# First FFN product in three token slices of 512 instead of four of 384

## The chip, the cores and the metric

The kernel runs on one core of one Trainium2 chip. The metric is the device time of one execution in microseconds (us), the median of three runs. About 0.2%, some 2 us, is what such a measurement can tell from no change.

## What is computed

An attention with a decaying state makes `x` (3072 tokens by 512). Two feed-forward blocks follow; the change touches the second one:

```python
def _moe2_ref(x, w_in, w_out):          # w_in 512 x 2048, w_out 2048 x 512
    h = x @ w_in
    g = h * (1.0 / (1.0 + np.exp(-1.702 * h)))
    return (g @ w_out).astype(np.float32)
```

## The kernel before

Two devices shape every matrix product. First, each operand is split into a high part, rounded to the fp32r format, and a low part that holds the rest, and one product is three matmuls: high by high, high by low, low by high (`mm3`; the profile's lines L259, L260, L261). Second, a two-by-two block product is done with seven block products instead of eight (P1 to P7, after Strassen and Winograd), which costs sums and differences on the vector engine (DVE).

The program runs in stages on the tensor engine (PE): attention and the first gates, the mixed weights, the "blend" (the first block's output, written to the spools `yd`), the expand stage (class `Expand`: `x @ w_in` and the gate, result to the spools `gd`), and the contract stage (`contract`: `g @ w_out`). The order on each engine is the order in which the Python code issues, so what stands before what is decided by hand.

Expand runs over token slices (`run`, L657), and in each over eight quads (`quad`, L630). A quad takes one column block of `w_in` (a "left operand": seven parts of 256 columns, each as high and low) and the slice's seven right operands, and makes the products in the order P1, P5, P4 of the quad before, P6, P2, P7, P3. Each product is six matmuls. ACT copies the sum out of PSUM after P1 (`s1`), P5 (`s5`), P6 (`u2`) and P7 (`u3`), and the next product on the same bank waits for that copy. DVE adds P2, P7 and P3 into `s1`, `u3`, `u2`. The generator `fourth` (L610) finishes the quad before: two gates on ACT (`g0`, `b12`) in front of P4, two behind it, four differences on DVE (L624), and a store to `gd`.

The seven right operands of a slice are made by the generator `operands` (L508): the slice's raw tokens are loaded, four differences are taken (`sub`), and `split` makes a high part (a cast) and a low part (a subtraction) for each of P1, P5, P6, P2, P7, P3, P4. `step(at)` in `run` moves it on by one part at places written as (quad, quarter): `NEXT0` and `NEXT` (L689, L690) in the slice before, and (0, 0), (0, 1) in the slice itself. Those of the first slice are made beside the blend (`ahead`).

Left operands sit in homes (`slot`, L558): left 0 in a home of its own, lefts 1 to 7 in seven others. As they fall free in the last slice, `OPENING` (L755) loads and splits the first operands of contract into them: `opening_slot`, `opening_split`, and `split_w` for the weights of P1. Contract has 21 turns of 48 matmuls, all of 512 columns; its loads from `gd` (`load`, L699) and its stores (`store`, L770) cut 512 tokens where a slice of 384 ends.

Of the kernel before, what the change touches and what calls it, by code (L numbers as in the profile page):

```python
# [16 lines left out]
P = 128  # L17
# [11 lines left out]
TS = 384  # L29
NS = NT // (2 * TS)  # L30
TU = 256
# [16 lines left out]
def tile_kernel(  # L48
# [36 lines left out]
    gd = spool("gd", NS, P, NQ, 7, TS)  # L85
# [413 lines left out]
    def load_y(raw, s):  # L499

        at = 0
        while at < 2 * TS:
            i, t0 = divmod(2 * TS * s + at, TB)
            n = min(TB - t0, 2 * TS - at)
            nc.sync.dma_start(raw[:, :, at : at + n], yd[i][:, :, t0 : t0 + n])
            at += n

    def operands(s, pool):  # L508

        raw = pool.tile([P, KD, 2 * TS], F32, tag="raw", name="yr")  # L510
        load_y(raw, s)
        (b11, b12), (b21, b22) = (
            [raw[:, 2 * k : 2 * k + 2, h * TS : (h + 1) * TS] for h in range(2)]
            for k in range(2)
        )
        x = right[s] = {}
        yield

        def split(name, b):
            hi, lo = (  # L520
                pool.tile([P, 2, TS], F32R, tag=f"y{w}", bufs=9, name=f"y{w}") for w in "hl"
            )
            nc.vector.tensor_copy(hi, b)
            nc.vector.tensor_tensor(lo, b, hi.bitcast(F32), ALU.subtract)
            x[name] = hi, lo

        def sub(out, a, b):
            nc.vector.tensor_tensor(out, a, b, ALU.subtract)

        t = pool.tile([P, 2, TS], F32, tag="t", name="yt")  # L530
        sub(t, b12, b11)
        sub(b12, b22, b12)
        yield
        split("P1", b11)
        yield
        split("P5", t)
        yield
        sub(t, b22, t)
        sub(b11, b21, t)
        yield  # L540
        split("P6", t)
        yield
        split("P2", b21)
        yield
        split("P7", b12)
        yield
        split("P3", b22)
        yield
        split("P4", b11)
        yield  # L550
# [4 lines left out]
    SLOT = "e", 0, 1, 4, 2, 3, 5, 6  # L555
    pools = {True: spare}

    def slot(n, shape):  # L558
        x = SLOT[n]
        return pools[x == "e"].tile(shape, F32R, tag=f"op{x}", name="op")  # L560
# [16 lines left out]
    class Expand:  # L577
# [4 lines left out]
        def bank(self, kind):  # L582
            bufs = {"a": 3, "e": 2, "c": 2}[kind]
            return self.ps.tile([P, TB], F32, tag=kind, bufs=bufs, name=kind)[:, :TS]

        def copy(self, ps, name):
            t = (
                self.ready.pop()
                if self.ready
                else self.p.tile([P, TS], F32, tag="s", bufs=6, name=name)  # L590
            )
            nc.scalar.copy(t, ps)
            return t

        def product(self, ps, name, s, j, start=False):
            xh, xl = right[s][name]
# [7 lines left out]
        def result(self, j):  # L604
            return [
                self.p.tile(shape, F32, tag=f"{tag}{j % 2}", name=tag)
                for tag, shape in (("g", [P, 7, TS]), ("b", [P, TS]))
            ]

        def fourth(self):  # L610
            a, s, j, g, b12, s1, u2, u3 = self.open
# [6 lines left out]
            for x, y, z in (  # L618
                (3, b12, g[:, 0]),
                (5, g[:, 2], b12),  # L620
                (4, g[:, 2], g[:, 3]),
                (6, g[:, 1], g[:, 4]),
            ):
                nc.vector.tensor_tensor(g[:, x], y, z, ALU.subtract)  # L624
# [5 lines left out]
        def quad(self, s, j, step):  # L630
            a, e, c = (self.bank(x) for x in "aec")
            g, b12 = self.results.pop(0) if self.results else self.result(j)
            self.product(a, "P1", s, j, True)
            s1 = self.copy(a, "s1")
# [20 lines left out]
            self.open = a, s, j, g, b12, s1, u2, u3  # L655

        def run(self):  # L657
            self.open = nxt = None
            for n in sorted(range(1, NQ), key=lambda n: SLOT[n]):
                left_tile(n)  # L660
            for n in range(1, NQ - 1):
                fetch_left(n, nc.sync)
            self.results = [self.result(0)]
            self.ready = [self.p.tile([P, TS], F32, tag="s", bufs=6, name="s1")]
            self.results.append(self.result(1))
            split_left(1, nc.vector.tensor_copy)
            for s in range(NS):

                for j in range(NQ):

                    def step(at):
                        nonlocal nxt
                        more = s + 1 < NS
                        if more and (j, at) == (2, 3):
                            nxt = operands(s + 1, self.py)
                            next(nxt)
                        elif more and (j, at) in (NEXT if s else NEXT0):
                            next(nxt)
                        elif s and (j, at) in ((0, 0), (0, 1)):
                            next(nxt)  # L680
                        if not more and (j, at) in OPENING:
                            for run in OPENING[j, at]:
                                run()

                    self.quad(s, j, step)
# [3 lines left out]
    NEXT0 = (4, 3), (6, 0), (6, 2), (6, 3), (7, 0), (7, 2), (7, 3)  # L689
    NEXT = (4, 3), (5, 1), (5, 3), (6, 3), (7, 0), (7, 2), (7, 3)  # L690
# [8 lines left out]
    def load(n, a, b, t):  # L699
        name, i = turns[n]  # L700
        low.setdefault(n, []).append((a, b, t))
        at = 0
        while at < TB:
            s, t0 = divmod(i * TB + at, TS)
            m = min(TB - at, TS - t0)
            nc.sync.dma_start(
                t[:, :, at : at + m].bitcast(F32),
                gd[s][:, a:b, RIGHT[name], t0 : t0 + m],
            )
            at += m  # L710
# [30 lines left out]
    def opening_slot(n):  # L741
        t = slot(n, [P, KH + 2, TB])
# [18 lines left out]
    for k, at in enumerate(  # L761
        ((3, 1), (3, 2), (3, 3), (4, 0), (4, 1), (4, 3), (5, 1), (5, 3))
# [3 lines left out]
    def contract(p, ps):  # L766
# [3 lines left out]
        def store(x, h, i, q, value):  # L770
            t = p.tile([P, TB], F32, tag="o", bufs=4, name="c")
            last = (x, h, i, q) == (1, 0, 2, 1)
            if not last:
                add(t, *value)
            at = 0
            while at < TB:
                s, t0 = divmod(i * TB + at, TS)
                m = min(TB - at, TS - t0)
                to = s * 2 * TS + h * TS + t0
                rows = slice((2 * x + q) * P, (2 * x + q + 1) * P)  # L780
                part = slice(at, at + m)
                if last:
                    add(t[:, part], *(v[:, part] for v in value))
                queue = nc.scalar if last and at else nc.sync
                queue.dma_start(out[rows, to : to + m], t[:, part])
                at += m

        u = [p.tile([P, 3, 2, TB], F32, name="ua")]
        for n, (name, i) in enumerate(turns):
# [4 lines left out]
            if name == "P5" and i == 0:  # L794
                u += [slot(x, [P, 3, 2, TB]).bitcast(F32) for x in (2, 3)]
# [12 lines left out]
            if i == 1 and r + 1 < 7:  # L808
                split_w(turns[n + 2][0], (7, 5)[r % 2])
# [146 lines left out]
    with tc.manual_schedule():  # L956
# [180 lines left out]
        def ahead(n):  # L1137
# [7 lines left out]
            elif early is None:  # L1145
# [4 lines left out]
                early = operands(0, py)  # L1150
# [14 lines left out]
        with tc.tile_pool(name="f", bufs=1, reuse_waits="tile") as pools[False]:  # L1165
# [6 lines left out]
            with (  # L1172
                tc.tile_pool(name="f2", bufs=1, side="right", reuse_waits="tile") as p2,
                tc.tile_pool(name="psf2", bufs=1, space=PSUM, reuse_waits="tile") as ps2,
            ):
                contract(p2, ps2)
# [100 lines left out]
```

## Time and profile before

| what | us |
|---|---|
| median of three runs (973.81 to 975.08) | 974.02 |
| the profiled execution | 973.11 |
| its span, first to last instruction | 971.3 |
| expand stage in it, first to first matmul of contract | 504.53 to 738.16 |
| contract stage, first to last matmul | 738.16 to 966.45 |

Matmuls are pipelined: the profile's duration of one is longer than the distance from one start to the next, and the second is what a stream costs. "Busy" of the tensor engine therefore also covers short waits; they are seen as larger distances between starts.

### The profile page before, as it was taken

Reading aid. Unit: us, or ns where it says so; the run is one execution under the profiler, and the core shown is the slowest. Engines: PE = TensorE matmul, PEld = TensorE weight load, DVE = VectorE, ACT = ScalarE, POOL = GpSimd, SP = SyncE. Lnnn points to the kernel's source line nnn. Section 1 sums busy time; section 2 is a strip of 40 time slices with the busy share of each in tenths; the row PEclk is TensorE's granted clock in tenths of the full one; section 3 lists DMA queues with packets and bytes.
Section 4 is the critical chain, followed back from the end, with each engine's and each line's share of the span. In section 5 each row is a group of like instructions: output and inputs, shape, how many; then the busy total and the mean of one; then the engine's idle time right before and its main releaser. Section 6 shows DMA issues by size and latency. Waiting matters only on the chain.

```text
span 971.3 us, 15570 instructions
## 1 busy us (share of the span) xinstructions
PE 952.3 (98%) x5992; PEld 826.0 (85%) x5992; DVE 719.3 (74%) x943; ACT 424.4 (44%) x691; POOL 229.4 (24%) x281
## 2 busy tenths in 40 slices
PE   6899999999999999999999999999999999999998
PEld 5678778888888888888889999999998888888886
DVE  6898878889889886766687976948686665566662
ACT  4555444433222222654536654554555544353430
POOL 6422100478787875330020000000000000000000
PEclk9999999999999999999999999999999999999999
DMA  9999766579898999899778546464696968767871
GB/s 349 400 350 350 281 214 202 199 246 359 314 365 288 357 338 395 306 334 312 248 254 305 226 171 246 203 250 184 253 348 252 339 222 271 254 196 230 290 233 50
DMA packets 112618, 266.74 MB, mean 275 GB/s; under 512 B 7872, under 2 KB 67264, under 8 KB 103456
## 3 DMA queue, kind: packets, MB, share of 16 engines
q1 hardware_dynamic: 96560, 186.64, 54.8%
q0 software_dynamic: 15840, 78.91, 21.4%
q8 instruction: 47, 0.77, 0.3%
q14 instruction: 27, 0.22, 0.1%
q10 hardware_dynamic: 144, 0.20, 0.1%
HBM read 164.53 MB, written 101.19 MB: 274 GB/s over the span
## 4 chain that ended last, share of the span: by engine, by line
PE 90%; DVE 4%; DMA 3%; issue 1%; ACT 1%; POOL 0%; DVEq 0%; POOLq 0%; ACTq 0%; SPq 0%
PE m L259 12%; PE m L260 12%; PE m L261 12%; PE psm L261 7%; PE psm L260 7%; PE psm L259 7%; PE a L260 4%; PE a L261 4%; PE a L259 4%; PE e L260 2%; PE e L259 2%; PE e L261 2%; PE psg L259 2%; PE y L442 2%; PE s L376 1%; DMA raw<-in_w_dram 1%
## 5 line engine op out<-in xcount | busy, mean ns | idle before, releaser
L260 PE MATMUL psm<-xl,wh 128*128 128x512 f32 x320 | 124.5, 389 | 0.0
L259 PE MATMUL psm<-xh,wh 128*128 128x512 f32 x320 | 124.5, 389 | 0.0
L261 PE MATMUL psm<-xh,wl 128*128 128x512 f32 x320 | 124.5, 389 | 0.0
L261 PE MATMUL m<-h,op 128*128 128x512 f32 x320 | 124.5, 389 | 0.0
L259 PE MATMUL m<-h,op 128*128 128x512 f32 x320 | 124.5, 389 | 0.0
L260 PE MATMUL m<-l,op 128*128 128x512 f32 x304 | 118.3, 389 | 0.0
L726 ACT CAST h<-l 128x2048 fp32r<-128x2048 f32 x38 | 72.3, 1914 | 85.1 <-PE m L261 56.9
L727 DVE TENSOR_TENSOR l<-l,h 128x2048 fp32r<-128x2048 f32 x38 | 85.7, 2286 | 22.5 <-ACT h L726 22.5
L732 POOL DMA_DIRECT2D op<-sw x6 | 3.2, 532 | 393.0 <-PE a L261 212.7
L260 PE MATMUL a<-yl,op 128*128 128x384 f32 x256 | 85.6, 335 | 0.1
L259 PE MATMUL a<-yh,op 128*128 128x384 f32 x256 | 85.5, 334 | 0.0
L261 PE MATMUL a<-yh,op 128*128 128x384 f32 x256 | 85.5, 334 | 0.0
L141 ACT ACTIVATE x<-raw 128x512 f32<-128x512 f32 x72 | 46.9, 675 | 70.3 <-DMA raw<-in_wo_dram 35.7
L261 PEld LDWEIGHTS m<-h,op 128*128 128x128 f32 x320 | 60.1, 188 | 12.6
L260 PEld LDWEIGHTS psm<-xl,wh 128*128 128x128 f32 x320 | 60.1, 188 | 12.6
L259 PEld LDWEIGHTS psm<-xh,wh 128*128 128x128 f32 x320 | 60.1, 188 | 12.5
L259 PEld LDWEIGHTS m<-h,op 128*128 128x128 f32 x320 | 60.1, 188 | 12.4
L261 PEld LDWEIGHTS psm<-xh,wl 128*128 128x128 f32 x320 | 60.1, 188 | 12.3
L260 PEld LDWEIGHTS m<-l,op 128*128 128x128 f32 x304 | 57.1, 188 | 11.8
L259 PE MATMUL m<-h,wh 128*128 128x512 f32 x168 | 65.4, 389 | 0.0
L261 PE MATMUL m<-h,wl 128*128 128x512 f32 x168 | 65.4, 389 | 0.0
L175 DVE TENSOR_TENSOR l<-l,h 128x2048 fp32r<-128x2048 f32 x19 | 43.6, 2292 | 26.1 <-ACT h L274 24.6
(172 smaller groups left out, 2198.1 us busy)
## 6 DMA issues: line engine op xcount, KB each, us to landing
gd<-g SPq DMA_DIRECT2D x32, 1344.0 KB, 5.0
qkv<-in_qkv_dram POOLq DMA_DIRECT2D x20, 1024.0 KB, 9.2
l<-gd SPq DMA_DIRECT2D x26, 768.0 KB, 7.4
l<-hd SPq DMA_DIRECT2D x19, 1024.0 KB, 7.4
raw<-in_w_dram SPq DMA_DIRECT2D x30, 512.0 KB, 5.9
hd<-g POOLq DMA_DIRECT2D x12, 1280.0 KB, 7.2
raw<-in_wo_dram SPq DMA_DIRECT2D x24, 512.0 KB, 6.8
l<-gd SPq DMA_DIRECT2D x24, 512.0 KB, 5.2
```

The lines of the kernel that those rows point to most:

```text
L141: nc.scalar.activation(x, high, AF.Abs, scale=2.0**16)
L175: nc.vector.tensor_tensor(lo, x, hi.bitcast(F32), ALU.subtract)
L259: nc.tensor.matmul(ps, wh, xh, start=start, stop=False, skip_group_check=True)
L260: nc.tensor.matmul(ps, wh, xl, start=False, stop=False, skip_group_check=True)
L261: nc.tensor.matmul(ps, wl, xh, start=False, stop=stop, skip_group_check=True)
L376: nc.tensor.matmul(self.s[u * D : (u + 1) * D, j, p, t], qkt[c][r, 1, p, u * D : (u + 1) * D], qkt[c][r, 0, p, t], start=True, stop=True, ...
L442: nc.tensor.matmul(out_y, vs[c][:, 2 * p + j, :], pt[c][:, j, p, :], start=(c % NCK == 0 and p < 2), stop=True, skip_group_check=True,)
L726: nc.scalar.copy(hi, x.bitcast(F32))
L727: nc.vector.tensor_tensor(x, x.bitcast(F32), hi.bitcast(F32), ALU.subtract)
L732: queue.dma_start(t.bitcast(F32), sw[PART[name]])
```

## The change

Expand works in three slices (`NS = 3`) of 512 tokens per half instead of four of 384. The raw tokens are loaded as four blocks into four tiles that are homes of low parts, and P1, P2, P7 and P3 leave their low parts there (`Homes` hands tags out and takes back those of the slice before). For the second and third slice the high parts are cast on ACT instead of DVE, in other places. Lefts 0 and 7 share one home, so each is fetched and split again (`FETCH`, `SPLIT`), and the order of the quads is `QUADS`. `g` is stored in two pieces of three and four parts. Contract's loads and stores need no cutting.

```diff
-TS = 384
-NS = NT // (2 * TS)
+NS = NT // (2 * TB)
...
-    def operands(s, pool):
+    def operands(s, copy, pool):
...
-            nc.vector.tensor_copy(hi, b)
+            htag, hi = ys_homes.tile("h")
+            tag, lo = low
+            copy(hi, b)
             nc.vector.tensor_tensor(lo, b, hi.bitcast(F32), ALU.subtract)
...
+        raws = [ys_homes.tile("l") for _ in range(4)]
+        b11, b12, b22, b21 = (whole(t) for t in raws)
+        for b, (k, h) in zip((b11, b12, b22, b21), ((0, 0), (0, 1), (1, 1), (1, 0))):
+            nc.sync.dma_start(b, yd[2 * s + h][:, 2 * k : 2 * k + 2])
+        yield
+        t, t7 = (pool.tile([P, 2, TB], F32, tag=f"yt{n}", name="yt") for n in range(2))
         sub(t, b12, b11)
         yield
+        sub(t7, b22, b12)
         yield
+        split("P1", b11, raws[0])
         yield
+        give("P1", "P5")
+        split("P5", t, ys_homes.tile("l"))
+        sub(t, b22, t)
         yield
+        split("P6", t, ys_homes.tile("l"))
+        sub(t, b21, t)
+        give("P6")
         yield
+        give("P2", "P7", "P3", "P4")
+        split("P2", b21, raws[3])
+        split("P7", t7, raws[1])
         yield
+        split("P3", b22, raws[2])
         yield
+        split("P4", t, ys_homes.tile("l"))
         yield
...
-    SLOT = "e", 0, 1, 4, 2, 3, 5, 6
+    SLOT = "e", 0, 1, 4, 2, 3, 5, "e", "w"
...
+            nc.sync.dma_start(gd[s][:, j, :3], g)
+            t = self.value("t", 4)
...
-            nc.sync.dma_start(gd[s][:, j], g)
-            if s == 0 and j == 0:
-                fetch_left(NQ - 1, nc.sync)
+            nc.sync.dma_start(gd[s][:, j, 3:], t)
+            if n in FETCH:
+                left_tile(FETCH[n])
+                fetch_left(FETCH[n], nc.sync)
...
-            if s == 0 and j + 2 < NQ:
-                split_left(j + 2)
+            if n in SPLIT:
+                split_left(SPLIT[n])
...
-                            nxt = operands(s + 1, self.py)
+                            nxt = operands(s + 1, nc.scalar.copy, self.py)
                             next(nxt)
-                        elif more and (j, at) in (NEXT if s else NEXT0):
+                        elif (more and at in NEXT) or (s and at in ((0, 0), (0, 1), (0, 2))):
                             next(nxt)
...
-    NEXT0 = (4, 3), (6, 0), (6, 2), (6, 3), (7, 0), (7, 2), (7, 3)
-    NEXT = (4, 3), (5, 1), (5, 3), (6, 3), (7, 0), (7, 2), (7, 3)
+    QUADS = range(NQ), range(NQ - 1, -1, -1), (0, 1, 2, 3, 7, 4, 5, 6)
+    FETCH = {0: 7, NQ: 0, 2 * NQ: 7}
+    SPLIT = {j: j + 2 for j in range(NQ - 2)} | {NQ + 4: 0, 2 * NQ + 2: 7}
+    NEXT = (4, 3), (5, 3), (6, 0), (7, 0), (7, 1)
...
-    OPENING = {(n + 1, 1): [lambda n=n: opening_slot(n)] for n in range(4)}
-    OPENING[5, 1] = [lambda: load_w("P1", 4)]
+    OPENING = {(n + 2, 1): [lambda n=n: opening_slot(n)] for n in range(3)}
+    OPENING[5, 1] = [lambda: opening_slot(3)]
+    OPENING[6, 1] = [lambda: load_w("P1", 4)]
     for n in range(2):
-        OPENING[6, 1 + 2 * n] = [
+        OPENING[7, 1 + 2 * n] = [
             lambda n=n: split_w("P1", 5, n * KH, n * KH + KH, nc.vector.tensor_copy)
```

How the order moves, at three places. First ACT in the first quad of the second slice (`yh` is a high part, `yl` holds a raw token block or a low part, `yt` a difference). Before:

```order
L592 COPY s5_5428<-e_5410 128x384
L602 ACTIVATE g_5333<-s1_5341 128x384
L602 ACTIVATE b_5334<-u2_5369 128x384
L592 COPY u2_5448<-a_5409 128x384
L602 ACTIVATE g_5333<-u3_5391 128x384
L602 ACTIVATE g_5333<-a_5330 128x384
L592 COPY u3_5474<-a_5409 128x384
```

Now:

```order
L607 COPY s5_5445<-e_5429 128x512
L617 ACTIVATE g1_5447<-s1_5358 128x512
L617 ACTIVATE b_5448<-u2_5389 128x512
L529 CAST yh_5457<-yl_5055 128x1024
L529 CAST yh_5460<-yt_5203 128x1024
L607 COPY u2_5469<-a_5428 128x512
L617 ACTIVATE g1_5447<-u3_5418 128x512
L617 ACTIVATE g1_5447<-a_5349 128x512
L529 CAST yh_5480<-yl_5054 128x1024
L607 COPY u3_5496<-a_5428 128x512
```

The casts for P2 and P7 stand between the gate `b` and the copy `u2`, and the one for P3 in front of `u3`. The second place is DVE at the same turn, from an add of the last quad of the first slice on. Before (P2's, P7's and P3's parts in this order):

```order
L650 TENSOR_TENSOR u3_5391<-u3_5391,s5_5349 128x384
L523 CAST yh_5394<-yr_5040 128x768
L524 TENSOR_TENSOR yl_5395<-yr_5040,yh_5394 128x768
L653 TENSOR_TENSOR u2_5369<-e_5331,u2_5369 128x384
L523 CAST yh_5405<-yr_5040 128x768
L524 TENSOR_TENSOR yl_5406<-yr_5040,yh_5405 128x768
L523 CAST yh_5438<-yr_5040 128x768
L524 TENSOR_TENSOR yl_5439<-yr_5040,yh_5438 128x768
L624 TENSOR_TENSOR g_5333<-b_5334,g_5333 128x384
```

Now, from the low part of P6 in that last quad on:

```order
L530 TENSOR_TENSOR yl_5400<-yt_5202,yh_5401 128x1024
L534 TENSOR_TENSOR yt_5202<-yl_5055,yt_5202 128x1024
L659 TENSOR_TENSOR s1_5358<-c_5351,s1_5358 128x512
L662 TENSOR_TENSOR u3_5418<-u3_5418,s5_5366 128x512
L665 TENSOR_TENSOR u2_5389<-e_5350,u2_5389 128x512
L530 TENSOR_TENSOR yl_5055<-yl_5055,yh_5457 128x1024
L530 TENSOR_TENSOR yl_5053<-yt_5203,yh_5460 128x1024
L636 TENSOR_TENSOR t_5474<-b_5448,g1_5447 128x512
L636 TENSOR_TENSOR t_5474<-g1_5447,b_5448 128x512
L636 TENSOR_TENSOR t_5474<-g1_5447,t_5474 128x512 x2
L530 TENSOR_TENSOR yl_5054<-yl_5054,yh_5480 128x1024
```

Both parts of P2 stood before the last add of the old slice, and those of P7 and P3 right behind it, all ahead of the gates' differences; now the low parts of P2 and P7 come after all three adds, and P3's after the four differences `t`. The third place is DVE at the end of expand, where the weights of contract's P1 are split in two halves. Before, both halves are done with a whole quad to come:

```order
L738 CAST op_7041<-op_6968 128x1024
L739 TENSOR_TENSOR op_6968<-op_6968,op_7041 128x1024
L624 TENSOR_TENSOR g_7000<-b_7001,g_7000 128x384
L624 TENSOR_TENSOR g_7000<-g_7000,b_7001 128x384
L624 TENSOR_TENSOR g_7000<-g_7000 128x384 x2
L647 TENSOR_TENSOR s1_7080<-c_7071,s1_7080 128x384
L650 TENSOR_TENSOR u3_7126<-u3_7126,s5_7088 128x384
L653 TENSOR_TENSOR u2_7104<-e_7070,u2_7104 128x384
```

Now they stand in the last quad itself, the second behind its last add:

```order
L744 CAST op_6596<-op_6521 128x1024
L745 TENSOR_TENSOR op_6521<-op_6521,op_6596 128x1024
L659 TENSOR_TENSOR s1_6559<-c_6552,s1_6559 128x512
L662 TENSOR_TENSOR u3_6612<-u3_6612,s5_6567 128x512
L665 TENSOR_TENSOR u2_6585<-e_6551,u2_6585 128x512
L744 CAST op_6596<-op_6521 128x1024
L745 TENSOR_TENSOR op_6521<-op_6521,op_6596 128x1024
```

## Rows read from the trace of the kernel before

**Rows 1.** Busy time by stretch: expand, then contract (columns named in the first row)

```profile
core 0: us, PE busy (x) PEld busy (x) DVE busy (x) ACT busy (x) POOL busy (x), PEclk, DMA share, GB/s
...
504.50:738.20 233.70, 233.59 (x1346) 232.98 (x1345) 175.70 (x301) 123.69 (x260) 1.44 (x3) 1.00 0.63 242
738.20:971.30 233.10, 228.64 (x1009) 188.97 (x1007) 132.85 (x96) 94.64 (x63) 2.65 (x5) 1.00 0.71 236
```

**Rows 2.** Timeline of PE: start, duration, engine, line, what; expand, then contract

```profile
504.53 0.33 PE L259 MATMUL a<-yh,op 128*128 128x384 f32 x1
...
555.69 0.33 PE L260 MATMUL e<-yl,op 128*128 128x384 f32 x1
...
567.99 0.34 PE L259 MATMUL e<-yh,op 128*128 128x384 f32 x1
...
571.35 0.34 PE L259 MATMUL a<-yh,op 128*128 128x384 f32 x1
571.80 0.44 PE L260 MATMUL a<-yl,op 128*128 128x384 f32 x1
572.08 0.34 PE L261 MATMUL a<-yh,op 128*128 128x384 f32 x1
...
738.16 0.39 PE L259 MATMUL m<-op 128*128 128x512 f32 x1
...
966.45 0.39 PE L261 MATMUL m<-h,op 128*128 128x512 f32 x1
```

**Rows 3.** Timeline of DVE at the first turn between slices

```profile
570.20 0.55 DVE L523 CAST yh<-yr 128x768 fp32r<-128x768 f32 x1
570.79 0.96 DVE L524 TENSOR_TENSOR yl<-yr,yh 128x768 fp32r<-128x768 f32 x1
571.66 0.55 DVE L647 TENSOR_TENSOR s<-c,s 128x384 f32<-128x384 f32 x1
```

**Rows 4.** Groups of ACT in expand: total us, mean ns of one

```profile
L592 ACT COPY u<-a 128x384 f32<-128x384 f32 x64 | 30.7, 480 | 41.5 <-PE a L261 41.5
L602 ACT ACTIVATE g<-u 128x384 f32<-128x384 f32 x32 | 17.0, 531 | 0.0
...
L726 ACT CAST h<-op 128x1024 fp32r<-128x1024 f32 x1 | 1.0, 1041 | 0.0
L953 ACT COPY c<-m 128x512 f32<-128x512 f32 x1 | 0.6, 589 | 2.1 <-PE m L261 2.1
```

**Rows 5.** Groups of DVE in expand

```profile
L624 DVE TENSOR_TENSOR g<-b,g 128x384 f32<-128x384 f32 x32 | 17.8, 555 | 28.1 <-ACT b L602 28.1
...
L753 DVE TENSOR_TENSOR op<-op 128x512 fp32r<-128x512 f32 x8 | 5.5, 692 | 0.3
...
L739 DVE TENSOR_TENSOR op<-op 128x1024 fp32r<-128x1024 f32 x2 | 2.5, 1225 | 0.1
L738 DVE CAST op<-op 128x1024 fp32r<-128x1024 f32 x2 | 1.4, 684 | 0.0
```

**Rows 6.** Timeline of ACT at the first turn

```profile
571.61 0.48 ACT L592 COPY s<-e 128x384 f32<-128x384 f32 x1 [0.56 <-PE e L261]
...
573.18 0.53 ACT L602 ACTIVATE b<-u 128x384 f32<-128x384 f32 x1 [0.40 <-DVE u L653]
574.04 0.48 ACT L592 COPY u<-a 128x384 f32<-128x384 f32 x1 [0.33 <-PE a L261]
574.41 0.53 ACT L602 ACTIVATE g<-u 128x384 f32<-128x384 f32 x1
```

**Rows 7.** DMA issues in expand: KB each, median us from issue to landing

```profile
gd<-g SPq DMA_DIRECT2D x31, 1344.0 KB, 5.0
op<-sp SPq DMA_DIRECT2D x4, 896.0 KB, 8.2
```

**Rows 8.** Timeline of DVE late in the blend, low part of its next operand

```profile
485.39 2.29 DVE L175 TENSOR_TENSOR l<-l,h 128x2048 fp32r<-128x2048 f32 x1 [1.63 <-ACT h L274]
```

**Rows 9.** Timeline of SP's queue at the end of expand

```profile
741.00 0.32 SPq L625 DMA_DIRECT2D gd<-g  x1
745.91 0.37 SPq L706 DMA_DIRECT2D l<-gd  x1
```

**Rows 10.** Timeline at the end of the program

```profile
966.88 0.76 DVE L768 TENSOR_TENSOR c<-m,ua 128x128 f32<-128x128 f32 x2 [4.75 <-PE m L261]
...
967.66 0.37 ACTq L785 DMA_DIRECT2D out_dram<-c  x1
```

More of the change, by code (lines that the diff above doesn't have):

```diff
@@ L84, in tile_kernel @@
     yd = spool("yd", NB, P, KD, TB)
-    gd = spool("gd", NS, P, NQ, 7, TS)
+    gd = spool("gd", NS, P, NQ, 7, TB)
     sp = spool("sp", NQ, P, 7 * 256)
@@ L497, in tile_kernel, with __init__, add, tile @@
     right = {}
[L499 to L506, printed above, removed]
-    def operands(s, pool):
[L510 to L515, printed above, removed]
-        x = right[s] = {}
[L517 to L522, printed above, removed]
-            nc.vector.tensor_copy(hi, b)
+    class Homes:
+        def __init__(self):
+            self.pools = {}
+            self.free = dict(l=[], h=[])
+        def add(self, pool, **counts):
+            for w, n in counts.items():
+                for _ in range(n):
+                    tag = f"y{w}{len(self.pools)}"
+                    self.pools[tag] = pool
+                    self.free[w].append(tag)
+        def tile(self, w):
+            tag = self.free[w].pop(0)
+            return tag, self.pools[tag].tile([P, 2, TB], F32R, tag=tag, name=f"y{w}")
@@ L524, in split, with give @@
+    ys_homes = Homes()
+    def operands(s, copy, pool):
+        x = right[s] = {}
+        used = {n: tags for n, (_, tags) in right.get(s - 1, {}).items()}
+        def give(*names):
+            for n in names:
+                for w, tag in zip("hl", used.get(n, ())):
+                    ys_homes.free[w].append(tag)
+        def split(name, b, low):
+            htag, hi = ys_homes.tile("h")
+            tag, lo = low
+            copy(hi, b)
             nc.vector.tensor_tensor(lo, b, hi.bitcast(F32), ALU.subtract)
-            x[name] = hi, lo
+            x[name] = (hi, lo), (htag, tag)
@@ L527, in sub, with whole @@
         def sub(out, a, b):
             nc.vector.tensor_tensor(out, a, b, ALU.subtract)
-        t = pool.tile([P, 2, TS], F32, tag="t", name="yt")
+        def whole(low):
+            return low[1].bitcast(F32)
+        raws = [ys_homes.tile("l") for _ in range(4)]
[4 more added lines that the diff above has]
+        t, t7 = (pool.tile([P, 2, TB], F32, tag=f"yt{n}", name="yt") for n in range(2))
@@ L553, in tile_kernel @@
     PART = dict(P1=0, P2=1, P4=2, P5=3, P6=4, P7=5, P3=6)
-    SLOT = "e", 0, 1, 4, 2, 3, 5, 6
-    pools = {True: spare}
+    SLOT = "e", 0, 1, 4, 2, 3, 5, "e", "w"
+    pools = {"e": spare}
     def slot(n, shape):
         x = SLOT[n]
-        return pools[x == "e"].tile(shape, F32R, tag=f"op{x}", name="op")
+        return pools.get(x, pools.get("f")).tile(shape, F32R, tag=f"op{x}", name="op")
     def left_tile(n):
@@ L583, in bank, with value, copy @@
             bufs = {"a": 3, "e": 2, "c": 2}[kind]
[L584 to L591, printed above, removed]
+            return self.ps.tile([P, TB], F32, tag=kind, bufs=bufs, name=kind)
+        def value(self, tag, *shape):
+            return self.p.tile([P, *shape, TB], F32, tag=tag, name=tag)
+        def copy(self, ps, tag):
+            t = self.value(tag)
             nc.scalar.copy(t, ps)
@@ L595, in product @@
         def product(self, ps, name, s, j, start=False):
-            xh, xl = right[s][name]
+            xh, xl = right[s][name][0]
             for k in range(2):
@@ L602, in gated @@
             nc.scalar.activation(x, c, AF.Gelu_apprx_sigmoid)
[L604 to L608, printed above, removed]
         def fourth(self):
-            a, s, j, g, b12, s1, u2, u3 = self.open
+            a, s, j, n, s1, u2, u3 = self.open
+            g, b12 = self.value(f"g{n % 2}", 3), self.value("b")
             self.gated(g[:, 0], s1)
@@ L617, in fourth, with quad @@
             self.gated(g[:, 1], a)
+            nc.sync.dma_start(gd[s][:, j, :3], g)
+            t = self.value("t", 4)
             for x, y, z in (
[L619 to L622, printed above, removed]
-            ):
-                nc.vector.tensor_tensor(g[:, x], y, z, ALU.subtract)
-            nc.sync.dma_start(gd[s][:, j], g)
-            if s == 0 and j == 0:
-                fetch_left(NQ - 1, nc.sync)
+                (0, b12, g[:, 0]),
+                (2, g[:, 2], b12),
+                (1, g[:, 2], t[:, 0]),
+                (3, g[:, 1], t[:, 1]),
+            ):
+                nc.vector.tensor_tensor(t[:, x], y, z, ALU.subtract)
+            nc.sync.dma_start(gd[s][:, j, 3:], t)
+            if n in FETCH:
+                left_tile(FETCH[n])
+                fetch_left(FETCH[n], nc.sync)
             yield
-        def quad(self, s, j, step):
+        def quad(self, s, j, n, step):
             a, e, c = (self.bank(x) for x in "aec")
-            g, b12 = self.results.pop(0) if self.results else self.result(j)
             self.product(a, "P1", s, j, True)
-            s1 = self.copy(a, "s1")
+            s1 = self.copy(a, f"s{n % 2}")
             self.product(e, "P5", s, j, True)
@@ L654, in quad @@
             step(3)
-            self.open = a, s, j, g, b12, s1, u2, u3
+            self.open = a, s, j, n, s1, u2, u3
         def run(self):
             self.open = nxt = None
-            for n in sorted(range(1, NQ), key=lambda n: SLOT[n]):
+            for n in sorted(range(1, NQ - 1), key=lambda n: SLOT[n]):
                 left_tile(n)
@@ L662, in run @@
                 fetch_left(n, nc.sync)
-            self.results = [self.result(0)]
-            self.ready = [self.p.tile([P, TS], F32, tag="s", bufs=6, name="s1")]
-            self.results.append(self.result(1))
+            for tag in ("s1", "s5", "u2", "u3", "s0", "b"):
+                self.value(tag)
+            for tag, m in (("t", 4), ("g0", 3), ("g1", 3)):
+                self.value(tag, m)
+            ys_homes.add(self.p, l=3, h=1)
             split_left(1, nc.vector.tensor_copy)
-            for s in range(NS):
-                for j in range(NQ):
+            for s, order in enumerate(QUADS):
+                for at_j, j in enumerate(order):
                     def step(at):
                         nonlocal nxt
+                        at = at_j, at
                         more = s + 1 < NS
-                        if more and (j, at) == (2, 3):
-                            nxt = operands(s + 1, self.py)
+                        if more and at == (2, 3):
+                            nxt = operands(s + 1, nc.scalar.copy, self.py)
                             next(nxt)
-                        elif more and (j, at) in (NEXT if s else NEXT0):
+                        elif (more and at in NEXT) or (s and at in ((0, 0), (0, 1), (0, 2))):
                             next(nxt)
[L679 to L682, printed above, removed]
+                        if not more:
+                            for run in OPENING.get(at, ()):
                                 run()
-                    self.quad(s, j, step)
+                    self.quad(s, j, s * NQ + at_j, step)
             for _ in self.fourth():
                 pass
-    NEXT0 = (4, 3), (6, 0), (6, 2), (6, 3), (7, 0), (7, 2), (7, 3)
-    NEXT = (4, 3), (5, 1), (5, 3), (6, 3), (7, 0), (7, 2), (7, 3)
+    QUADS = range(NQ), range(NQ - 1, -1, -1), (0, 1, 2, 3, 7, 4, 5, 6)
+    FETCH = {0: 7, NQ: 0, 2 * NQ: 7}
+    SPLIT = {j: j + 2 for j in range(NQ - 2)} | {NQ + 4: 0, 2 * NQ + 2: 7}
+    NEXT = (4, 3), (5, 3), (6, 0), (7, 0), (7, 1)
     RIGHT = dict(P1=0, P2=1, P3=2, P5=3, P6=4, P7=5, P4=6)
@@ L741, in opening_slot @@
     def opening_slot(n):
-        t = slot(n, [P, KH + 2, TB])
+        t = slot((1, 2, 3, 7)[n], [P, KH + 2, TB])
         if n < 2:
@@ L772, in store @@
             last = (x, h, i, q) == (1, 0, 2, 1)
[L773 to L786, printed above, removed]
+            to = (2 * i + h) * TB
+            rows = slice((2 * x + q) * P, (2 * x + q + 1) * P)
+            for part in (slice(0, 384), slice(384, TB)) if last else (slice(0, TB),):
+                add(t[:, part], *(v[:, part] for v in value))
+                queue = nc.scalar if last and part.start else nc.sync
+                queue.dma_start(out[rows, to + part.start : to + part.stop], t[:, part])
         u = [p.tile([P, 3, 2, TB], F32, name="ua")]
@@ L794, in contract @@
             if name == "P5" and i == 0:
-                u += [slot(x, [P, 3, 2, TB]).bitcast(F32) for x in (2, 3)]
+                u += [slot(x, [P, 3, 2, TB]).bitcast(F32) for x in (3, 7)]
             pq = [ps.tile([P, TB], F32, tag="m", bufs=6, name="m") for _ in range(2)]
@@ L808, in contract @@
             if i == 1 and r + 1 < 7:
-                split_w(turns[n + 2][0], (7, 5)[r % 2])
+                split_w(turns[n + 2][0], (8, 5)[r % 2])
             for q, m in enumerate(pq):
@@ L1149, in ahead @@
                 )
-                early = operands(0, py)
+                ys_homes.add(py, l=8, h=7)
+                early = operands(0, nc.vector.tensor_copy, py)
                 next(early)
@@ L1163, in tile_kernel @@
         first.close()
-        with tc.tile_pool(name="f", bufs=1, reuse_waits="tile") as pools[False]:
+        with tc.tile_pool(name="f", bufs=1, reuse_waits="tile") as pools["f"]:
             with (
@@ L1175, in tile_kernel @@
             ):
+                pools["w"] = p2
                 contract(p2, ps2)
```

23 lines of the change are left out of this document (2 added, 21 removed).

## The prediction

> **What bounds the kernel now.** I read the stretches first. In expand PE is busy 233.59 of 233.70 us, DVE 175.70, ACT 123.69, at a granted clock of 1.00 [rows 1]: PE sets the time, DVE has a quarter to spare. Busy time hides short waits, so I read PE's starts next [rows 2]. From 555.69 to 567.99 lie 71 starts, 12.30 us: a 384-column matmul costs 0.1732 us. In contract, 1008 matmuls of 512 columns go from 738.16 to 966.45: 228.29 over 1007 steps, 0.2267 us each. Expand's 1344 matmuls would need 232.8 us; they take 738.16 - 504.53 = 233.6. The rest is waits: at 571.35 the next start comes 0.45 later instead of 0.17, and the one behind it 0.28 later, so a wait also costs some 0.1 of resuming. What it waits for is on DVE [rows 3]: the low part of P4 starts at 570.79, lasts 0.96, ends at 571.75, and the matmul that reads it starts 0.05 later. So already now, where the slice turns, the operands come just too late. This is the place to look at.
>
> **Fewer matmuls.** 128 columns more cost 0.0535 us, 0.418 ns each, so 384 columns are 160 ns and some 13 ns belong to each instruction. The columns stay the same (4 x 384 = 3 x 512), 336 instructions go: 1008 x 0.2267 = 228.5 us, against the 233.6 of today **-5.1 us**, with the old waits in it. The Trainium skill ("TensorE: Matmul & The Clock Gate", Back-to-back issue gap) gives a warm gap of N / 2.4 + 2.5 ns for isolated matmuls; by that the 336 instructions are worth an estimated 0.8 us, not 4.5. Both of my pitches are measured in streams of this kernel, so they decide.
>
> **The turn between slices.** A product is now 6 x 0.2267 = 1.36 us, a quad seven of them, 9.52. Durations: ACT casts 128x1024 in 1.04, copies 512 columns in 0.59; a gate of 384 takes 0.53 against 0.48 for a copy, so I estimate 0.64 at 512 [rows 4]. DVE takes 1.23 for 128x1024, 0.69 for 512 columns, 0.68 for a 1024 cast [rows 5]. An ACT copy starts 0.26 after the product's last step (571.35, 571.61) [rows 2, 6]. The next operation on ACT starts 0.1 before the end of the one ahead (574.04 + 0.48 against 574.41) [rows 6], on DVE 0.08 (570.79 + 0.96 against 571.66), or 0.04 after it where it needs its result (570.20 + 0.55 against 570.79) [rows 3].
>
> Last quad of the old slice, from its start: P5 ends at 2.72, so ACT copies `s5` at 2.97, gates from 3.45 to 4.6, casts P5's high part 4.53 to 5.57. DVE makes its low part 5.60 to 6.83, the next difference to 7.97, the four `t` from 7.88 to 10.5 (the last reads the one ahead of it, 0.1 more), P6's low part 10.42 to 11.65, the last difference to 12.78, then the adds into `s1` at 12.70, `u3` at 13.31, `u2` at 13.92 to 14.61. That is **5.09 after the new slice's first quad has started**, since this quad holds four operations of 1.23 us for the operands beside its own eight.
>
> First quad of the new slice, from its start. PE: P1, P5, the old P4, P6, and P2 due at 5.44. ACT: the gate `b` needs `u2`, so 5.13 to 5.77 (as now it waits for DVE at 573.18 [rows 6]); then P2's cast 5.67 to 6.71, P7's 6.61 to 7.65, the copy `u2` to 8.14, two gates, P3's cast 9.1 to 10.1. DVE: P2's low part 6.74 to 7.97, P7's to 9.11, four `t` from 9.03 to 11.65, P3's low part 11.57 to 12.80. So on PE:
>
> - P2's first matmul waits for the high part from 5.44 to 6.76: 1.3 us.
> - Its second, due at 6.99, waits for the low part to 8.02: 1.0 us. P2 ends at 9.15. P7 finds its parts and `u2` there and ends at 10.51.
> - P3's first starts at 10.51; its second, due at 10.74, waits for the low part to 12.85: 2.1 us. P3 ends at 13.98, not 9.52.
>
> With 0.1 of resuming twice a turn costs 4.7 us, two turns **+9.3 us**. Bounds from below: if the gates' lateness and the `t` block came away entirely (ACT free to cast at 4.5, low part at 5.6 to 6.8), P2 would still lose 1.2 us a turn, +2.4. From above: 0.3 us of extra hand-over at each of five steps of the chain, +12. I take the chain, all from durations of this trace.
>
> P4's low part, late today, follows P3's, is ready some 1.1 us into the second quad and due at 2.7; so it costs nothing, and DVE has caught up by that quad's end.
>
> **The end of expand.** The second half of P1's weights is split in the last quad behind its last add: the four `t` end at 8.86, first half 8.78 to 10.72, adds to 12.55, second half 12.47 to 14.41. Contract begins at 9.52 + 1.36 = 10.88 and reads that low part in its fifteenth matmul, at 14.05: **+0.5 us** with resuming (0 to 1). The first store piece of the last `g` goes out at about 3.4 after contract's start, the load of the third turn stands behind the `t` piece, at 6.1, and behind the first's landing, at 8.4. Today it is issued 7.75 after 738.16 and 4.9 after the store [rows 9]; its reader is two turns of 10.9 us away, so nothing.
>
> **What I cost at nothing.** The operands of the first slice are made beside the blend by DVE as before, a third longer, two splits at once in one step: 3.8 us instead of 1.5 against an idle of 1.63 [rows 8], so one low part of the blend starts some 0.6 later; without that cover 0 to 0.7. Lefts 0 and 7 are loaded twice more, 8.2 us each [rows 7]. The tight one, 7 in the third slice, is issued 8.9 into the second quad and lands 7.6 into the third, where ACT would cast it at 7.2; the copy `u3` behind it is due at 12.2, so a landing up to 10 is hidden. Contract loads the same bytes in fewer pieces. At the end the 384 columns are now added and stored before the 128: both adds take the same 0.76 and only the last store, on ACT's queue, is smaller [rows 10]; 0 to -0.3.
>
> **Sum.** -5.1 + 9.3 + 0.5 = +4.7 us. The profiled execution (973.11, 1.8 outside its span) would be 977.8; it stood 0.9 under the median of 974.02, so I forecast **978.7**.
>
> **Rivals.**
> 1. *The cover holds.* PE runs through both turns, as it does today at the turns behind the first. For it: DVE is idle a quarter of the stage [rows 1], and the high parts that ACT now casts give it more. Against: the work is piled into one quad, and today's first turn shows a wait with less of it. -5.1 + 0.5 = -4.6: 969.4. Chance 0.07. It decides against me if P2's low part is there within 5.7 us of the turn.
> 2. *Half the wait.* The chain's links overlap more than rows of 384 say, say P2 waits 1.2 us and P3 1.0: 2 x 2.3 = 4.6, sum 0, 974.0. Chance 0.09.
> 3. *Transfers add waits.* There is one tile `t` where each `g` had its own seven parts in two buffers. In a plain quad it is written last at 8.9 and first again 5.3 us later; a store of 1344 KB lands in 5.0 [rows 7]. Beyond some 7 us DVE falls behind by the excess in every quad. With five quads of the last slice, beside contract's first loads, 0.8 too slow, 4 us more: 982.7. Chance 0.09.
> 4. *The instructions' fixed part does not come back*, a matmul costing 4/3 of 0.1732 us here: 1008 x 0.2309 = 232.8, only the 0.8 of waits saved, 983.0. Chance 0.02, as 0.2267 is measured over 1007 steps of contract.
>
> **How the numbers follow.** The forecast, long waits at both turns, has 0.73. Its bounds reach from 971.3 (2.4 at the turns, nothing elsewhere) to 982.6 (12, 1 at the end, 0.7 in the blend), the middle of that being likeliest. Range 975.0 to 981.5: it holds all but a tenth of the forecast, half of case 2 and half of case 3, 0.75 to 0.8 together; wider would only take in case 1. About 0.2%, 1.9 us, is what a measurement can tell. Faster by more is case 1 and a little of case 2, 0.09; the same is most of case 2, 0.08; slower the rest, 0.83.
>
> **What would show it.** PE's starts in expand 0.2267 apart; in the first quad of the second and of the third slice gaps of about 1.3 and 1.0 us at P2 and 2.1 at P3's second matmul, with ACT's cast and DVE's low part ending 0.05 before; elsewhere in expand none; one of 0.4 in contract's fifteenth matmul. Expand from first matmul to contract's first in some 237.8 us. It would be wrong if the high part of P2 is cast before the gate `b`, or if DVE's adds of the last quad end within it.

## The result and the profile after

The changed kernel takes 980.28 us (median of six, 979.58 to 981.67), the kernel before 973.91 in six: a ratio of 1.0065, 95% interval 1.0052 to 1.0078. Slower by 6.4 us, where 4.7 were forecast. The interval leaves 1 out, so the loss is real.

The profiled execution took 981.67, its span is 979.8, 8.5 more than before. Four differences make that up: expand starts at 505.00, not 504.53 (+0.5), lasts 240.62 us to contract's first matmul at 745.62, not 233.63 (+7.0), contract lasts 230.12 to its last matmul at 975.74, not 228.29 (+1.8), and the tail behind is 4.06, not 4.85 (-0.8). PE's timeline now, first of expand, first and last of contract:

```profile
505.00 0.39 PE L257 MATMUL a<-yh,op 128*128 128x512 f32 x1
...
745.62 0.47 PE L257 MATMUL m<-op 128*128 128x512 f32 x1
...
975.74 0.39 PE L259 MATMUL m<-h,op 128*128 128x512 f32 x1
```

The busy time by stretch (expand, then a piece behind the second turn; columns as in [rows 1]):

```profile
505.00:745.60 240.60, 231.79 (x1009) 189.85 (x1008) 152.81 (x210) 129.41 (x211) 1.08 (x2) 0.99 0.62 237
675.10:678.50 3.40, 3.40 (x10) 2.63 (x9) 2.59 (x4) 0.00 (x0) 0.00 (x0) 0.51 0.52 212
```

DVE is less busy than before, 152.81 us against 175.70 [rows 1], and yet PE now waits for it. PE's timeline at the first turn between slices shows where (its first row is the new slice's first matmul):

```profile
579.80 0.39 PE L257 MATMUL a<-yh,op 128*128 128x512 f32 x1
...
585.01 0.39 PE L259 MATMUL a<-yh,op 128*128 128x512 f32 x1
587.20 0.51 PE L257 MATMUL c<-yh,op 128*128 128x512 f32 x1 [1.80 <-ACT yh L529]
588.46 0.51 PE L258 MATMUL c<-yl,op 128*128 128x512 f32 x1 [0.76 <-DVE yl L530]
588.80 0.40 PE L259 MATMUL c<-yh,op 128*128 128x512 f32 x1
...
591.09 0.39 PE L257 MATMUL e<-yh,op 128*128 128x512 f32 x1
593.33 0.50 PE L258 MATMUL e<-yl,op 128*128 128x512 f32 x1 [1.85 <-DVE yl L530]
593.67 0.39 PE L259 MATMUL e<-yh,op 128*128 128x512 f32 x1
```

The waits are the distances between starts, less the 0.2267 of a matmul: P2's first (bank `c`) 1.96, its second 1.03, P3's second (bank `e`) 2.01, and 0.11 of resuming twice. That is 5.2 us where the old turn had 0.6, 0.4 of it in [rows 2] at P4 and 0.2 at P3. The same comes at the second turn, and there something follows that was not forecast:

```profile
666.45 0.39 PE L259 MATMUL a<-yh,op 128*128 128x512 f32 x1
668.63 0.50 PE L257 MATMUL c<-yh,op 128*128 128x512 f32 x1 [1.79 <-ACT yh L529]
669.89 0.50 PE L258 MATMUL c<-yl,op 128*128 128x512 f32 x1 [0.76 <-DVE yl L530]
...
672.52 0.39 PE L257 MATMUL e<-yh,op 128*128 128x512 f32 x1
674.76 0.50 PE L258 MATMUL e<-yl,op 128*128 128x512 f32 x1 [1.86 <-DVE yl L530]
675.10 0.58 PE L259 MATMUL e<-yh,op 128*128 128x512 f32 x1
675.48 0.63 PE L257 MATMUL e<-yh,op 128*128 128x512 f32 x1
675.90 0.63 PE L258 MATMUL e<-yl,op 128*128 128x512 f32 x1
...
678.04 0.63 PE L257 MATMUL a<-yh,op 128*128 128x512 f32 x1
678.47 0.44 PE L258 MATMUL a<-yl,op 128*128 128x512 f32 x1
678.75 0.40 PE L259 MATMUL a<-yh,op 128*128 128x512 f32 x1
```

The starts from 675.48 to 678.47 are 0.43 apart: the clock is at 1.2 instead of 2.4 GHz (granted clock 0.51 in the stretch above). Nine steps from 675.10 take 3.65 us instead of 2.04, 1.6 lost. So 228.5 + 5.2 + 5.2 + 1.6 = 240.5 of the measured 240.6: expand is accounted for. ACT and DVE at the first turn:

```profile
584.58 0.59 ACT L607 COPY s<-e 128x512 f32<-128x512 f32 x1 [2.63 <-DVE u L662]
585.06 0.63 ACT L617 ACTIVATE g<-s 128x512 f32<-128x512 f32 x1
585.59 0.62 ACT L617 ACTIVATE b<-u 128x512 f32<-128x512 f32 x1
586.11 1.03 ACT L529 CAST yh<-yl 128x1024 fp32r<-128x1024 f32 x1
```

```profile
583.80 0.68 DVE L662 TENSOR_TENSOR u<-u,s 128x512 f32<-128x512 f32 x1
584.40 0.68 DVE L665 TENSOR_TENSOR u<-e,u 128x512 f32<-128x512 f32 x1
587.17 1.23 DVE L530 TENSOR_TENSOR yl<-yl,yh 128x1024 fp32r<-128x1024 f32 x1 [2.09 <-ACT yh L529]
588.32 1.22 DVE L530 TENSOR_TENSOR yl<-yt,yh 128x1024 fp32r<-128x1024 f32 x1
589.45 0.68 DVE L636 TENSOR_TENSOR t<-b,g 128x512 f32<-128x512 f32 x1
...
592.06 1.22 DVE L530 TENSOR_TENSOR yl<-yl,yh 128x1024 fp32r<-128x1024 f32 x1
```

The turn's first matmul starts at 579.80. DVE's last add of the old slice ends 5.3 us behind that (5.09 forecast), P3's low part 13.5 behind (12.80 forecast). The forecast did not see the first row of ACT: the copy `s5` waits 2.63 us for the add (L662) that reads the old `s5`, since there is now one tile for it and there were six for all copies. The gate `b` starts 0.5 after the add into `u2` has ended, and all behind it is late against the forecast by as much or more.

At contract's start the two halves of P1's weights are late:

```profile
742.25 0.69 DVE L636 TENSOR_TENSOR t<-b,g 128x512 f32<-128x512 f32 x1 [4.17 <-DMA gd<-t]
```

```profile
745.93 0.40 PE L258 MATMUL m<-op 128*128 128x512 f32 x1
746.85 0.50 PE L259 MATMUL m<-op 128*128 128x512 f32 x1 [0.53 <-DVE op L745]
...
749.60 0.40 PE L258 MATMUL m<-op 128*128 128x512 f32 x1
750.52 0.50 PE L259 MATMUL m<-op 128*128 128x512 f32 x1 [0.53 <-DVE op L745]
```

The differences `t` wait for the store of the same tile, and the weights' split stands behind them: with resuming, 0.9 us are lost at contract's third matmul and again at its fifteenth. DVE waits for such a store in eight quads of this profile, 1.5 to 4.4 us each; PE loses time by it only here.

### The profile page after: what moved, and what is told of

Its sections match the earlier page's. It is cut to its first block, busy times and chain, and to the rows that moved or that the text cites. A ratio compares the mean times of both kernels' runs of the same rounds, so it can differ in the third digit from the quotient of the medians.

```text
span 979.8 us, 14573 instructions
## 1 busy us (share of the span) xinstructions
PE 950.6 (97%) x5656; PEld 782.1 (80%) x5656; DVE 706.9 (72%) x857; ACT 430.7 (44%) x643; POOL 227.7 (23%) x281
## 4 chain that ended last, share of the span: by engine, by line
PE 86%; DVE 6%; DMA 4%; ACT 2%; issue 1%; POOL 0%; DVEq 0%; POOLq 0%; ACTq 0%; SPq 0%
PE m L259 12%; PE m L258 12%; PE m L257 12%; PE psm L257 7%; PE psm L258 7%; PE psm L259 7%; PE a L257 4%; PE a L258 4%; PE a L259 4%; DMA qkv<-in_qkv_dram 2%; PE e L258 2%; PE e L259 2%; PE e L257 2%; PE psg L257 2%; PE y L440 1%; DMA raw<-in_w_dram 1%
## 5 line engine op out<-in xcount | busy, mean ns | idle before, releaser
L257 PE MATMUL a<-yh,op 128*128 128x512 f32 x192 | 75.2, 392 | 0.0
L258 PE MATMUL a<-yl,op 128*128 128x512 f32 x192 | 75.0, 391 | 0.0
L259 PE MATMUL a<-yh,op 128*128 128x512 f32 x192 | 74.9, 390 | 0.0
```

Of the source, the lines that this page charges most:

```text
L257: nc.tensor.matmul(ps, wh, xh, start=start, stop=False, skip_group_check=True)
L258: nc.tensor.matmul(ps, wh, xl, start=False, stop=False, skip_group_check=True)
L259: nc.tensor.matmul(ps, wl, xh, start=False, stop=stop, skip_group_check=True)
```

## The experiments

All are edits of the changed kernel unless it is said otherwise. The question was whether the loss is the two turns, what in the turns sets it, and whether fewer matmuls saved what was forecast.

**Without the operand work of the later slices.**

```diff
-            xh, xl = right[s][name][0]
+            xh, xl = right[0][name][0]
...
-                            nxt = operands(s + 1, nc.scalar.copy, self.py)
...
```

> Leaves out all operand work of the second and third slice (no loads of raw tokens, no differences, no splits there); their quads read the first slice's operands. My theory, that the time is lost at the two turns to late operands and that fewer matmuls do save: no gap in expand at all, expand 1008 x 0.2267 = 228.5 us from its first matmul to contract's first (240.6 in the changed kernel), time about 968 to 970, some 4 to 5 under the kernel before. Rival, that matmuls of this stage or its transfers are slower by themselves: expand stays above 232, time above 973.

Measured: 969.03 us, ratio to the kernel before 0.9951 (0.9931 to 0.9970). PE, first matmul of expand and first of contract:

```profile
505.34 0.39 PE L257 MATMUL a<-yh,op 128*128 128x512 f32 x1
...
733.82 0.39 PE L257 MATMUL m<-op 128*128 128x512 f32 x1
```

228.48 us, no gap in between, as expected. The fewer matmuls save 5.1 us against 233.63, and all that is lost in expand goes away with the operand work. Slower matmuls are out as a rival, and so are the transfers that are left, the stores of `g` and the loads of left operands. The loads of the raw tokens went with the operands; the spread operands below keep them.

**Two tiles for `s5`.**

```diff
-            g, b12 = self.value(f"g{n % 2}", 3), self.value("b")
+            g, b12 = self.value("g", 3), self.value("b")
...
-            s5 = self.copy(e, "s5")
+            s5 = self.copy(e, f"s5{n % 2}")
...
```

> Two tiles for s5 instead of one (room made by one tile g instead of two). Theory: at each turn ACT's copy s5 waits 2.6 us for DVE's add that reads the old s5, and this makes P2's first wait 1.96 instead of the 1.3 forecast. So the copy starts at 0.26 after P5, the gate b then waits for u2, P2's first wait falls by 0.6 to 0.7, expand by 1.3 us, time to about 979. Rival: the copy's wait is covered by the gate's wait for u2 anyway, gaps and time unchanged (980.3).

Measured: 980.66 (1.0041 to 1.0083 of before), where about 979 was expected. The wait of the copy for the add is gone, and now the adds themselves hold ACT (the last row is DVE's add into `u2`):

```profile
583.00 0.59 ACT L607 COPY s<-e 128x512 f32<-128x512 f32 x1 [0.77 <-PE e L259]
584.25 0.64 ACT L617 ACTIVATE g<-s 128x512 f32<-128x512 f32 x1 [0.67 <-DVE s L659]
585.40 0.63 ACT L617 ACTIVATE b<-u 128x512 f32<-128x512 f32 x1 [0.52 <-DVE u L665]
```

```profile
584.69 0.68 DVE L665 TENSOR_TENSOR u<-e,u 128x512 f32<-128x512 f32 x1
```

P2's first wait is 1.50, 0.46 less, not the 0.6 to 0.7 expected: the gate `b` now starts as the add ends, and the add itself is 0.2 later than forecast. The time did not fall. The single tile is a link of the chain, a short one.

**Two tiles `t`** (with `b` kept in `t[:, 2]`, one tile `g`).

> Two tiles t instead of one, b kept inside t and one tile g (for room). Theory: the four differences wait for the store of the same tile (24.3 us in 8 waits), which delays the second split of P1's weights in the last quad, and with it contract's first matmuls. Those waits on the store vanish, contract's two gaps of 0.69 fall to none at the third matmul and about 0.4 at the fifteenth, time 1.0 to 1.3 us less, about 979. The gaps at the turns stay 1.96, 1.04 and 2.0. Rival, that the store's wait is also part of the turns: their gaps shrink by over 0.3 each.

Measured: 980.57. No wait of `t` for its store is left in expand, and contract shows one gap, 0.46 at the fifteenth matmul, as expected; its duration is 228.85. The time did not fall to the 979 expected. P2's first and P3's second wait at the first turn grew by 0.2 each where they were to stay, because keeping `b` in `t` makes each of the four differences wait for the one ahead (starts 0.79 apart in place of 0.60), and the clock was low at both turns; expand took 241.38. So the store's wait costs only at contract's start. It is not always that long: in the next experiment, whose code is the same as the changed kernel's up to the last store, it was 1.6 us there and cost nothing.

**The last store cut as before.**

```diff
-            for part in (slice(0, 384), slice(384, TB)) if last else (slice(0, TB),):
+            for part in (slice(0, 128), slice(128, TB)) if last else (slice(0, TB),):
```

> Only the very last store is cut as before: 128 columns first, the 384 last on ACT's queue. From the last matmul's start to the end of the span 4.06 us in the changed kernel, 4.85 before. If the smaller last piece is what saved it: 4.8 again, time 0.8 more (981). If it was one run's landing: 4.1 and no change.

Measured: 980.66, tail 979.9 - 975.87 = 4.03. So the order of the last two pieces does nothing. A second profile of the kernel before was taken to see whether its longer tail comes again:

> The kernel before once more, for a second profile of it. From the last matmul's start to the end of the span it showed 4.85 us, the changed kernel and five experiments 4.03 to 4.08, also the one whose last store is cut as before. If the 0.8 us belong to the kernel before, 4.8 again (then the many cut stores ahead are the likeliest cause); if it was one landing, 4.1. Expand 233.6 and the gap of 0.45 at P4 of the first turn should come again, the first matmul of expand anywhere from 504 to 508.

Its time was 973.94; its last matmul starts at 967.50, its span is 972.2, the tail 4.70. So the 0.7 to 0.8 us belong to the kernel before. Its last piece, 192 KB on ACT's queue, landed 2.5 and 2.3 us after its issue in the two profiles; the same piece, issued equally soon after the last matmul, took 1.9 in the experiment above. That is 0.6 and 0.4 of the difference. Why it lands later in the kernel before, behind many cut stores, was not tried. Its gaps at the first turn came again, and expand took 739.21 - 505.55 = 233.66.

**Idle matmuls in the waits.** They write a spare bank that nobody reads.

```diff
+            self.fill(s, j, n, 13)
             self.product(c, "P2", s, j, True)
...
+            self.fill(s, j, n, 9)
             self.product(e, "P3", s, j)
```

> The changed kernel with idle matmuls into a spare PSUM bank at each turn: 13 (2.95 us) in front of P2 and 9 (2.04 us) in front of P3, where PE waits anyway. Theory: the clock falls to 1.2 GHz because PE is idle there, in one or both turns of a run, for 12 to 16 matmuls of 0.43 us, some 2 to 3 us each time that is not hidden behind P3's wait. With PE kept busy no matmul of 0.43 is left, expand 238.5 to 239.5 in place of 240.6, and the time 1 to 3 us less: 977.5 to 979.5, with less scatter. Rival, the low clock has nothing to do with the waits: matmuls of 0.43 are still there and the time is 980 or more.

Measured: 979.60 (1.0043 to 1.0073 of before), just above the 977.5 to 979.5 expected. The windows over both turns, all at full clock:

```profile
586.00:600.00 14.00, 14.00 (x62) 11.21 (x61) 8.93 (x11) 9.14 (x15) 0.00 (x0) 1.00 0.33 132
668.00:682.00 14.00, 14.00 (x62) 11.16 (x62) 9.36 (x12) 8.65 (x14) 0.00 (x0) 1.00 0.32 132
```

No matmul of 0.43 is left, and expand is 239.06, 1.6 less than in the changed kernel's profile, as expected. In the median the gain is 0.7, within the scatter; so that the waits bring the low clock is shown by the profiles, and what it costs in the median is not. The low clock follows the waits in every profile: the six profiles in which the turns' waits stay (the changed kernel, two tiles `s5`, two tiles `t`, the cut store, and the two experiments that follow) show it, the changed kernel's at one turn, the others at both. Those without operand work, with the waits filled, or with the operands spread show it at none.

**P2's and P7's casts in front of the gates.**

```diff
-            next(fourth)
-            step(0)
+            if n in (NQ, 2 * NQ):
+                step(0)
+                next(fourth)
+            else:
+                next(fourth)
+                step(0)
```

> At the two turns the step with P2's and P7's casts is issued in front of the old quad's gates g and b instead of behind them. Theory, ACT's order is one link: P2's cast follows the copy s5 at once, 1.05 us earlier, so P2's first gap falls from 2.19 to about 1.1 and P3's low part comes some 0.9 earlier; expand 1.9 us less in two turns. Rival, DVE alone sets the turn: P2's gap falls but P3's grows by as much, expand unchanged.

Measured: 979.69 (1.0043 to 1.0091). P2's first wait falls from 1.96 to 0.91 at the first turn and 1.27 at the second, its second stays 1.03, P7 waits a little for `u2`, P3 for both its parts; a turn sums to 4.4 and 4.8 in place of 5.2. The 1.9 us less that were expected did not come: in this profile the clock fell at both turns behind P3 and took the gain back, and expand is 241.06. ACT's order is a link, not the cause.

**High parts cast on DVE again, in the new places.**

```diff
-                            nxt = operands(s + 1, nc.scalar.copy, self.py)
+                            nxt = operands(s + 1, nc.vector.tensor_copy, self.py)
```

> The high parts of the second and third slice are cast on DVE again, in the places of the change. Theory, DVE's load in one quad is the root: DVE ends its adds 1.3 us later, P2's parts and then P7's and P3's come one after the other on DVE, the sum of gaps per turn is 5 to 6.5 us (5.2 in the changed kernel), time 980 to 983. Rival, ACT's casts behind the gates are the root: without them the gaps shrink below 3.5 per turn and the time is under 977.

Measured: 981.10 (1.0055 to 1.0096). The waits move to P3, whose two first matmuls now wait for DVE in turn:

```profile
588.61 0.39 PE L259 MATMUL a<-yh,op 128*128 128x512 f32 x1
590.78 0.75 PE L257 MATMUL e<-yh,op 128*128 128x512 f32 x1 [1.78 <-DVE yh L529]
592.04 0.80 PE L258 MATMUL e<-yl,op 128*128 128x512 f32 x1 [0.51 <-DVE yl L530]
592.63 0.63 PE L259 MATMUL e<-yh,op 128*128 128x512 f32 x1
```

With P2's 0.7 and P7's 0.5 a turn sums to about 4.3, without what the low clock adds: less than the 5 to 6.5 expected. The low clock behind P3 at both turns makes it up (expand 241.42). Which engine casts does not decide.

**The same work in other places.**

```diff
+        if s:
+            split("P7", t7, raws[1])
+            yield
...
-        split("P7", t7, raws[1])
+        if not s:
+            split("P7", t7, raws[1])
...
-    NEXT = (4, 3), (5, 3), (6, 0), (7, 0), (7, 1)
+    NEXT = (4, 3), (5, 3), (6, 0), (6, 2), (7, 0), (7, 1), (7, 3)
```

> P7's split moved into the sixth quad of the slice before (one more home for a high part, room by one tile g), P2's to the last step of that slice, P3's to the first of the new one. Nothing but places changes. Theory: at the turn one split is left in front of the gates' differences, so P2 waits 0.6 to 1.3, P3 not at all, the clock stays up, expand 230 to 232, time 970 to 972, under the kernel before. Rival, it is not the place but the amount of the operand work: the wait moves to another product and the sum of gaps per turn stays above 4 us, time above 978.

Measured: 971.46, ratio to before 0.9975 (0.9965 to 0.9984). Expand is 230.92; at each turn 0.9 at P2 and 0.25 at P7 are left with resuming, nothing at P3, and the granted clock is 1.00 throughout. So the places decide, with the amount of operand work and the loads of raw tokens unchanged. Contract lost time here too, as in the changed kernel's profile (229.81 us): the store of `t` held DVE for 3.87 us in the last quad, and its third and fifteenth matmuls came late:

```profile
736.80 0.50 PE L259 MATMUL m<-op 128*128 128x512 f32 x1 [0.32 <-DVE op L749]
...
740.46 0.50 PE L259 MATMUL m<-op 128*128 128x512 f32 x1 [0.53 <-DVE op L749]
```

**These places, with two tiles `s5` and the weights' split earlier.**

```diff
...
-        OPENING[7, 1 + 2 * n] = [
+        OPENING[7, n] = [
```

> The one before plus two tiles s5 and P1's weights split a step and two earlier in the last quad. Theory: P2 waits 0.3 to 1.0 at each turn, contract starts without a gap of 0.4 or more, time 969 to 971, 3 to 5 us under the kernel before. If the gap at contract's fifteenth matmul stays, the transfer of the weights and not DVE's order sets it.

Measured: 969.61, ratio 0.9962 (0.9949 to 0.9974), the best of all. All that is left at a turn, and the start of contract:

```profile
584.94 0.39 PE L257 MATMUL c<-yh,op 128*128 128x512 f32 x1
585.98 0.50 PE L258 MATMUL c<-yl,op 128*128 128x512 f32 x1 [0.65 <-DVE yl L530]
586.31 0.40 PE L259 MATMUL c<-yh,op 128*128 128x512 f32 x1
...
735.07 0.39 PE L257 MATMUL m<-op 128*128 128x512 f32 x1
735.29 0.39 PE L258 MATMUL m<-op 128*128 128x512 f32 x1
```

P2's second matmul waits 0.8 at either turn; contract's first matmuls follow each other without a gap, as its weights are split ahead of the differences. Expand is 230.37, contract 228.25.

## Why the prediction was right, and where it was short

*Fewer matmuls, -5.1.* Right: 228.48 us in the experiment without later operands.

*The turns, +9.3.* The mechanism is right to the matmul: waits at P2's first and second and at P3's second, forecast 1.3, 1.0 and 2.1, measured 1.96, 1.03 and 2.01. The term was short by the first of them: 5.2 a turn instead of 4.7. The chain left out that `s5` has one tile; ACT's copy waits for an add that the same overloaded quad delays. Two tiles took 0.46 of the 0.66 away. The other 0.2 is DVE's last add, which ends 5.28 behind the turn's start and not 5.09: the chain let the differences behind P5's and P6's low parts start 0.08 before those end, and they start 0.03 after (for P6's, 580.81 + 1.22 against 582.06), as each overwrites the tile that the low part reads. (That quad holds seven operations of its own beside the operands', four `t` and three adds, not eight; the chain itself lists seven.)

*Not in the sum: the clock.* With PE waiting 1.96 + 1.03 and 2.01 us between 666.45 and 674.76, the clock fell to 1.2 GHz, worth 1.6 in the profiled run; at the first turn the same waits left it at 1.00. The prediction named no such term. With PE kept busy through the waits it did not come.

*The end of expand, +0.5.* 0.57 in seven of the experiments' profiles (0.46 at the fifteenth matmul and 0.11 of resuming), 1.8 in the changed kernel's own and 1.6 with the spread operands, when a store of `t` held DVE 4.17 and 3.87 us. That is the mechanism of rival 3, the one tile `t`, in one place: in the other quads DVE waited up to 4.4 us for a store without a gap on PE.

*At nothing:* the blend shows no gap with its longer operand steps, the reload of lefts 0 and 7 none either. Where expand starts varies with the stages before it, from 504.09 to 508.12 in the profiles of the edits, so the 0.5 in this run is no effect of the change. The tail gained 0.7 to 0.8, forecast 0 to -0.3.

By the profiled runs: -5.1 + 10.5 + 1.6 + 1.8 - 0.8 + 0.5 (the later start) = 8.5. The medians differ by 6.4; of the 2.1 between, the late store explains 1.2 and the later start 0.5 in that run. That the forecast came within 1.7 of the median is in part luck: the tail's gain, which was not forecast at that size, hid part of what the turns and the clock cost beyond the sum. Rival 1, that the cover holds, fell at the turns. The last experiment comes near its time, 969.6 against the 969.4 worked out for it, but by other terms: 0.9 at each turn, nothing at contract's start, and the shorter tail.

## What to carry to other kernels

An engine that is busy only two thirds of a stage can still be the bound where a schedule piles its work into one step: work through that step in order, on each engine, with every link to the other engines, before placing anything by the average. In such a chain count the buffers too: a value that used to rotate through several tiles and now has one adds a wait of its own. And larger matmuls gain only their fixed part, here some 13 ns each, 4.4 us over 336 of them; two turns with late operands took back 10.5.

## What was not expected of the hardware

A few waits of 1 to 2 us close together in an otherwise busy stream of matmuls were followed by a lower granted clock (0.51 over 3.4 us), which nearly doubled the distance of starts, from 0.23 to 0.43 us, for some ten matmuls. In which turn, and behind which wait, changed from run to run: the experiment with the last store cut as before, the same code up to there, had it behind P2 at the first turn and behind P3 at the second. Where the slow matmuls fell in front of another wait, part of their cost was hidden: with two tiles `s5` the clock fell behind P2 at both turns, and P3's wait shrank to 0.4 and 0.6.
